# Chunk-select attention into soft MoE on one core: regrouped score blocks, a rearranged last batch, spare matmuls, and a second expert product in halves

## The chip, the core and the metric

The kernel runs on one core of a Trainium2 chip. A core has a matrix engine (TensorE, PE in the profile, with its weight loads shown apart as PEld), a vector engine (VectorE, DVE), a scalar engine (ScalarE, ACT), GpSimd (POOL) and SyncE (SP), which run their own instruction streams and wait for each other through semaphores. PE writes only to PSUM; DVE and ACT bring results from PSUM to SBUF. Sixteen DMA engines move data between HBM and SBUF. The metric is device time in microseconds (us) of one execution. Before the change it was 175.84 us (median of 3 runs, 175.56 to 177.19).

## The reference, cut to what matters

Attention over 4 batches x 8 heads of 768 rows and 64 columns, where each query row keeps only the 6 chunks of 32 keys with the largest upper bound of its score, followed by a soft mixture of experts over the 3072 x 512 result (8 experts, 4 slots each, hidden width 1024).

```python
k_min, k_max = k_chunks.min(3), k_chunks.max(3)             # 24 chunks of 32 keys
ub = sum(maximum(q * k_min, q * k_max))                     # per query row and chunk, causal
sel = top 6 chunks of ub
scores = where(sel & causal, scale * q @ k.T, -1e9)
attn = softmax(scores);  x = (attn @ v) as rows of (batch, position), 512 wide
logits = x @ phi                                            # 3072 x 32 slots
d = softmax of logits over the 3072 rows;  slot_input = d.T @ x
slot_out[e] = relu(slot_input[e] @ w1[e]) @ w2[e]           # 8 experts
c = softmax of logits over the 32 slots
out = c @ slot_out                                          # 3072 x 512, float32
```

## The kernel before

The work is a hand-written order (`manual_schedule`): each engine runs its instructions as the program lists them.

**The pair loop.** Two heads make a pair; there are 16 pairs, four per batch. Iteration `i` computes scores and exponentials of pair `i`, the upper bounds and the selection of pair `i+1`, the transposes of k and q of pair `i+2`, the product with v (`pv`) of pair `i-1`, and the normalised rows (`normalise`, `x_transposes`, `evac_x`) of pair `i-2`. The loads of k and q run four pairs ahead, those of v two pairs ahead, all of them and the expert weights as DMAs issued by POOL on one queue, so they land in the order of issue. Each `load_w` brings 1 MB (as it lies in SBUF), each k, q or v load 192 KB; `wplan` says how many weights an iteration issues. Weights 0 to 7 are of the first expert product and 8 to 15 of the second.

**Scores.** Because of causality a key block `kg` of 128 keys meets only the query blocks from `kg` on. `GROUPS` packs these blocks into six score tiles (`scores(i, g)`), each followed by one exponential on ACT (`expo`, line 297) and one `affine_select` on POOL (line 299) for the diagonal block. The score tiles rotate through two PSUM buffers of the pool `p_sc` (tag `sc`): a group's matmuls (line 272 for q and k, line 283 for the selection mask) wait until the exponential two groups earlier has read its buffer. Before the change the widths are 512, 512, 512, 512, 512 and 128 query columns per head. Results lie in `ep` (9 buffers) and, for the last group, `ep5`. `p_tp` (two buffers of one bank) and `p_at` (one of two banks) hold all other PSUM tiles.

**The soft MoE of a batch.** Once a batch's four pairs are transposed, PE computes its `moe_logits`, DVE copies them and takes a maximum per slot (`moe_copy`), PE transposes it (`moe_max`), DVE reduces it (`moe_bound`), PE spreads it over the partitions (`moe_exp`, first matmul), DVE updates the running maximum `m_run` and subtracts it (line 400), ACT takes the exponential `d_sb` (line 404), and PE adds up the slot inputs (`moe_dispatch`, line 435). `moe_comb` and `moe_ct` make the transposed combine weights. For batches 0 to 2 this is spread over the following loop iterations; for the last batch it stands alone behind the loop.

**The tail.** `pv` of the last pair is split into query blocks 0 to 3 and 4 to 5. After the last dispatch DVE writes the slot inputs (`siT_pad`), PE runs `experts_in` (line 617: four experts side by side, 128 x 32 weights, 512 columns), ACT the relu, PE the transposes `hidden_T`, then `experts_out` (line 652) into `so_ps` with `normalisers` (lines 638 and 640: 24 sums for the combine weights and one for the slot sums) between its halves, ACT `so_sb` (line 669), and 24 output products (line 680) that DVE and ACT scale by `cinv` and SP stores.

Of the kernel before, what the change touches and what calls it, by code (L numbers as in the profile page):

```python
# [18 lines left out]
CH = 32  # L19
# [12 lines left out]
    [(1, 0, 512, 0)],  # L32
    [(2, 0, 512, 0)],
    [(4, 0, 256, 0), (0, 512, 256, 256)],
    [(3, 0, 384, 0), (1, 512, 128, 384)],
    [(5, 0, 128, 0)],
]
# [9 lines left out]
def kernel(  # L47
# [60 lines left out]
    tp2 = i_ctx.enter_context(tc.tile_pool(name="tp2", bufs=2, side="right"))  # L108
    ep = i_ctx.enter_context(tc.tile_pool(name="ep", bufs=9, side="right"))
    ep5 = i_ctx.enter_context(tc.tile_pool(name="ep5", bufs=2, side="right"))  # L110
    tpu = u_ctx.enter_context(tc.tile_pool(name="tpu", bufs=2, side="right"))
# [61 lines left out]
    load_v(1)  # L173
    nc.gpsimd.dma_start(out=phi_sb, in_=moe_phi.rearrange("(hg p) s -> p hg s", p=P))
    make_identity(nc, identf)


# [113 lines left out]
    def expo(i, g):  # L291
        w = WIDTH[g]
        if g < 5:
            e = ep.tile([P, 2, 512], BF16, name="e_sb", tag="e_sb")
        else:
            e = ep5.tile([P, 2, P], BF16, name="e5_sb", tag="e5_sb")
        nc.scalar.activation(e[:, :, :w], st.pop(("scps", i, g))[:, :, :w], func=ACT.Exp, scale=scale)  # L297

        nc.gpsimd.affine_select(  # L299
            out=e[:, :, :P], in_=e[:, :, :P], compare_op=ALU.is_ge, fill=0.0,  # L300
            base=0, pattern=[[0, 2], [1, P]], channel_multiplier=-1,
        )
        st["e", i, g] = e

    def pv(i, ts):
        if i == LAST and ts[0] in (0, 4):
            st["at", i] = p_sc.tile([P, 2, 512], F32, name="at_ps", tag="sc")
        elif ts[0] == 0:
            st["at", i] = p_at.tile([P, 2, 512], F32, name="at_ps", tag="at")
        at = st["at", i]  # L310
        for t in ts:
            for h in range(2):
                o = at[:, h, t * (D + 1):(t + 1) * (D + 1)]
                for kg in range(t + 1):
                    g, c = BLOCK[(kg, t)]
                    nc.tensor.matmul(  # L316
                        o, lhsT=st["e", i, g][:, h, c:c + P], rhs=v_t[i % NV][:, h, kg, :],
                        start=(kg == 0), stop=(kg == t),
                    )

    def normalise(i, t0=0, t1=NQT, at=None):
        b, j = divmod(i, NPB)
        at = st.pop(("at", i)) if at is None else at
        at = at[:, :, :NQT * (D + 1)].rearrange("p h (t d) -> p h t d", t=NQT)[:, :, t0:t1]
        if j == 0:
            st["x", b] = xp.tile([P, NQT, H, D], BF16, name="x_sb", tag="x_sb")
        inv = tp2.tile([P, 2, NQT, 1], F32, name="inv", tag="inv")[:, :, t0:t1]
        nc.vector.reciprocal(inv, at[:, :, :, D:D + 1])
        nc.vector.tensor_tensor(  # L329
            st["x", b][:, t0:t1, 2 * j:2 * j + 2, :].rearrange("p t h d -> p h t d"),  # L330
            at[:, :, :, :D], inv.broadcast_to([P, 2, t1 - t0, D]), op=ALU.mult,
        )
# [18 lines left out]

    def moe_logits(b, hgs=range(NDG), home=(p_tp, "tp")):
        if hgs[0] == 0:
            st["lgps", b] = home[0].tile([P, NQT, NS], F32, name="lg_ps", tag=home[1])
        ps, xT = st["lgps", b], st["xT", b]
        for t in range(NQT):
            for hg in hgs:
                nc.tensor.matmul(
                    ps[:, t, :], lhsT=xT[:, hg, t * P:(t + 1) * P], rhs=phi_sb[:, hg, :],
                    start=(hg == 0 and t == 0), stop=(hg == NDG - 1 and t == NQT - 1),  # L360
                )

    def moe_copy(b):
        lg = small.tile([P, NQT, NS], F32, name="lg", tag="lg")
        pm = small.tile([P, NS], F32, name="pm", tag="pm")
        ps = st.pop(("lgps", b))
        if b == B - 1:
            nc.vector.tensor_reduce(pm, ps.rearrange("p t s -> p s t"), axis=AX.X, op=ALU.max)
            nc.scalar.copy(lg, ps)
        else:  # L370
            nc.vector.tensor_copy(lg, ps)
            nc.vector.tensor_reduce(pm, lg.rearrange("p t s -> p s t"), axis=AX.X, op=ALU.max)
        st["lg", b], st["pm", b] = lg, pm
# [14 lines left out]
    def moe_exp(b):  # L388
# [17 lines left out]
        if b > 0:  # L406

            dm = small.tile([P, 1, NS], F32, name="dm", tag="dm")
            nc.vector.tensor_tensor(dm[:, 0, :], m_old, m_new, op=ALU.subtract)
            nc.scalar.activation(dm, dm, func=ACT.Exp)  # L410
            if b == B - 1:
                moe_comb(b)
            nc.vector.tensor_tensor(si_acc, si_acc, dm.broadcast_to([P, NDG + 1, NS]), op=ALU.mult)
# [50 lines left out]
    wplan = {i: 1 for i in range(-1, NPAIR)}  # L464
    for i in (2, 5, 8, 11):
        wplan[i] = 0
    for i in (12, 13):
        wplan[i] = 2
    nw = 1
# [7 lines left out]
    for i in range(-2, NPAIR):  # L477
# [15 lines left out]
        if have(i + 1):  # L493
            select(i + 1)
        if have(i + 2):
            transposes(i + 2, "k")
# [17 lines left out]
        if have(i - 1):  # L514
            pv(i - 1, [3])
        if have(i + 2):
# [12 lines left out]
        if have(i):  # L529
            scores(i, 4)  # L530
            expo(i, 4)
            scores(i, 5)
            expo(i, 5)
        if have(i + 1) and i >= 0:
            ns_transposes(i + 1)
            evac_ns(i + 1)
        if have(i - 1):
            pv(i - 1, [4])
        moe(moe_dispatch, i - 3)
        if have(i - 1):  # L540
            pv(i - 1, [5])
# [17 lines left out]
    siT_pad = pads.tile([P, NDG, E, CH], BF16, name="siT_pad")  # L559
    hT_pad = pads.tile([P, NFG, E, CH], BF16, name="hT_pad")  # L560
    normalise(LAST - 1)
    pv(LAST, [0, 1, 2, 3])
    at_a = st["at", LAST]
    x_transposes(LAST - 1)
    evac_x(LAST - 1, copy=nc.scalar.copy)
    normalise(LAST, 0, 4, at_a)
    pv(LAST, [4, 5])
    moe_logits(B - 1, range(NDG - 1), (p_at, "at"))
    x_transposes(LAST, 0, 4)
    evac_x(LAST, 0, 4, nc.scalar.copy)  # L570
    normalise(LAST, 4, NQT)
    x_transposes(LAST, 4, NQT)
    evac_x(LAST, 4, NQT)
    moe_logits(B - 1, range(NDG - 1, NDG))
    nc.gpsimd.memset(siT_pad, 0.0)
    nc.gpsimd.memset(hT_pad, 0.0)
    i_ctx.close()
    moe_copy(B - 1)
    moe_max(B - 1)
    moe_bound(B - 1)  # L580
    moe_exp(B - 1)
    moe_dispatch(B - 1)


    tail = ctx.enter_context(tc.tile_pool(name="tail", bufs=1))
    op = ctx.enter_context(tc.tile_pool(name="op", bufs=5))
# [10 lines left out]
    for g in range(2):  # L597
# [5 lines left out]
        )  # L603
    moe_ct(B - 1)
    cinv = tail.tile([P, B * NQT], F32, name="cinv")
# [3 lines left out]
    h_sb = tail.tile([P, 2, 512], BF16, name="h_sb")  # L609
    so_sb = tail.tile([P, Dm], BF16, name="so_sb")  # L610
    h_ps = [p_sc.tile([P, 2, 512], F32, name=f"h_ps{f}", tag="sc") for f in range(2)]

# [21 lines left out]

    def normalisers():
        ps = p_tp.tile([P, B * NQT + 1], F32, name="cs_ps", tag="tp")
        for n in range(B * NQT):
            nc.tensor.matmul(
                ps[:, n:n + 1], lhsT=cT[:, n // 2, n % 2], rhs=ones_sq[:, :1], start=True, stop=True)
        nc.tensor.matmul(  # L640
            ps[:, B * NQT:], lhsT=zrow.rearrange("p j s -> p (j s)"), rhs=identf[:1, :1], start=True, stop=True)
        nc.vector.reciprocal(zinv, ps[:, B * NQT:])
        nc.vector.reciprocal(cinv, ps[:, :B * NQT])

    so_ps = p_at.tile([P, 2, 512], F32, name="so_ps", tag="at")

    def experts_out(f):
        for g in range(2):
            for fg in range(f * 4, (f + 1) * 4):
                for j in range(4):  # L650
                    e = g * 4 + j
                    nc.tensor.matmul(  # L652
                        so_ps[j * CH:(j + 1) * CH, 0, :], lhsT=hT_pad[:, fg, e, :],
                        rhs=w_sb[E + e][:, fg * Dm:(fg + 1) * Dm],
                        start=(g == 0 and fg == 0), stop=(g == 1 and fg == NFG - 1),
                    )

    experts_in(0, 0)
    experts_in(0, 1)
    relu(0)  # L660
# [3 lines left out]
    relu(1)  # L664
    experts_out(0)
    hidden_T(1)
    normalisers()
    experts_out(1)
    nc.scalar.activation(so_sb, so_ps[:, 0, :], func=ACT.Copy, scale=zinv)

# [3 lines left out]
    for m in range(B * NQT // 2):  # L674
        o_sb = op.tile([P, 2, Dm], F32, name="o_sb", tag="o_sb")
        rows = out[m * 2 * P:(m + 1) * 2 * P, :].rearrange("(p x) d -> p x d", x=2)
        for x in range(2):
            pool, tag = homes[n % 5]
            o_ps = pool.tile([P, Dm], F32, name="o_ps", tag=tag)
            nc.tensor.matmul(o_ps, lhsT=cT[:, m, x], rhs=so_sb, start=True, stop=True)  # L680
            if x == 0:
                nc.vector.tensor_scalar_mul(o_sb[:, x, :], o_ps, cinv[:, n:n + 1])  # L682
# [37 lines left out]
```

## Time and profile before

| | |
|---|---|
| median of 3 runs | 175.84 us |
| profiled execution | 176.33 us, of which 174.6 us from the first to the last instruction |
| busy time | PE 136.6 us (78%), DVE 124.8 (71%), ACT 120.5 (69%), POOL 98.8 (57%) |
| DMA | 26.25 MB in on the queue that POOL feeds, 6.29 MB out |
| chain that ended last, by engine | PE 36%, ACT 21%, DMA 15%, DVE 14%, POOL 6% |

The chain is followed back from the last instruction: at each step to whatever released it, or to the instruction before it on its engine. The execution has four stages. Up to about 14.8 us the first pairs are loaded and transposed. From 14.82 us (first exponential) to 134.54 us (end of the last) the pair loop runs, about 6.85 us for a pair without MoE work. From there to 156.20 us the tail runs from the last `pv` to the first store. The last 18.4 us are the stores. A line of the timeline below has start, duration, engine, source line, operation, tiles and count; the bracket behind it is how long the engine sat idle before it and what released it. A wait line has the time in total, the number of waits and the longest.

### The profile page before, as it was taken

What the parts mean: (1) busy time and instruction counts of PE and PEld (TensorE: products, weight loads), DVE (VectorE), ACT (ScalarE), POOL (GpSimd) and SP (SyncE); (2) the same over time, 40 slices, a digit from 0 to 9 for tenths busy, and PEclk for the clock granted to TensorE, in tenths of its full rate; (3) what the DMA queues carried; (4) which work ended last, traced back from release to release, by engine and by line L of the source; (5) the groups of instructions that cost most, each with busy time, mean ns of one, the idle gap of its engine ahead of it and who ended that gap; (6) DMA issues with size and microseconds to landing.
All of it is one profiled execution on the core that took longest, in us unless ns stands there. A gap on an engine that the chain in (4) does not pass through costs nothing.

```text
span 174.6 us, 6281 instructions
## 1 busy us (share of the span) xinstructions
PE 136.6 (78%) x2629; PEld 100.3 (57%) x2630; DVE 124.8 (71%) x430; ACT 120.5 (69%) x163; POOL 98.8 (57%) x192
## 2 busy tenths in 40 slices
PE   0459698999799789999988899999688669976410
PEld 0346476777577568877776777777567543532100
DVE  3467869999689888999987899999653560247530
ACT  2356998988789678988977698897667321156430
POOL 7995869869578457877775586659345500000000
PEclk9999999999999999999999999999999956999855
DMA  3999999999999999999999999199999994009995
GB/s 48 164 152 187 190 211 195 211 196 206 184 208 197 209 190 158 211 167 207 168 144 207 182 202 148 14 186 212 197 213 216 216 215 88 4 8 400 406 403 226
DMA packets 40460, 32.94 MB, mean 189 GB/s; under 512 B 26352, under 2 KB 34544, under 8 KB 40432
## 3 DMA queue, kind: packets, MB, share of 16 engines
q0 software_dynamic: 38416, 26.25, 102.4%
q1 hardware_dynamic: 2016, 6.29, 9.1%
q8 instruction: 20, 0.33, 0.7%
q14 instruction: 8, 0.07, 0.1%
HBM read 52.49 MB, written 6.29 MB: 337 GB/s over the span
## 4 chain that ended last, share of the span: by engine, by line
PE 36%; ACT 21%; DMA 15%; DVE 14%; POOL 6%; issue 4%; SPq 0%; ACTq 0%; POOLq 0%; DVEq 0%
ACT e_sb L297 14%; DMA k_in<-in_k_dram 10%; PE sc_ps L272 6%; DMA out_dram<-o_sb 5%; PE tr_ps L184 4%; PE sc_ps L283 4%; PE at_ps L316 4%; PE h_ps L617 3%; ACT kT L193 3%; POOL e_sb L299 3%; PE ub_ps L231 2%; DVE x_sb L329 2%; PE so_ps L652 2%; PE ub_ps L227 2%; DVE mm L202 2%
## 5 line engine op out<-in xcount | busy, mean ns | idle before, releaser
L297 ACT ACTIVATE e_sb<-sc_ps 128x1024 bf16<-128x1024 f32 x96 | 83.7, 937 | 10.5 <-PE sc_ps L283 10.5
L299 POOL TENSOR_SCALAR_AFFINE_SELECT e_sb<-e_sb 128x256 bf16<-128x256 bf16 x96 | 39.4, 422 | 33.5 <-ACT e_sb L297 32.9
L272 PE MATMUL sc_ps<-qT,kT 64*128 64x512 bf16 (+3 forms) x256 | 39.7, 310 | 7.6 <-ACT e_sb L297 7.4
L283 PE MATMUL sc_ps<-nsT,smask 64*128 64x256 bf16 (+1 forms) x448 | 37.1, 245 | 0.0
L316 PE MATMUL at_ps<-v_t,e_sb 128*128 128x65 bf16 x672 | 29.4, 194 | 1.1 <-DVE x_sb L329 1.1
L283 PEld LDWEIGHTS <-smask 64*128 64x128 bf16 x448 | 23.0, 95 | 7.3 <-issue 0.5
L316 PEld LDWEIGHTS <-e_sb 128*128 128x128 bf16 x672 | 25.1, 98 | 2.9 <-DVE x_sb L329 1.1
L272 PEld LDWEIGHTS <-kT 64*128 64x128 bf16 x256 | 15.4, 94 | 13.3 <-issue 8.3
L243 DVE MAX8 mx<-ub_ps 128x8 f32<-128x8 f32 (+2 forms) x192 | 17.0, 161 | 6.1 <-PE ub_ps L231 5.0
L202 DVE TENSOR_REDUCE mm<-kT 128x24 bf16<-128x768 bf16 x16 | 15.2, 951 | 6.1 <-ACT kT L193 5.1
L134 POOL DMA_DIRECT2D v_t<-in_v_dram x16 | 16.7, 1046 | 2.0 <-PE ns_ps L254 1.3
L193 ACT COPY kT<-tr_ps 128x768 bf16<-128x768 bf16 x16 | 12.8, 803 | 6.0 <-PE tr_ps L184 5.9
L329 DVE TENSOR_TENSOR x_sb<-at_ps,inv 128x768 bf16<-128x768 f32 (+2 forms) x17 | 15.5, 911 | 0.6
L208 DVE TENSOR_REDUCE mm<-kT 128x24 bf16<-128x768 bf16 x16 | 15.1, 942 | 0.0
L184 PE MATMUL tr_ps<-ident,k_in 128*64 128x128 bf16 x192 | 9.4, 240 | 7.1 <-DMA k_in<-in_k_dram 6.1
L193 ACT COPY qT<-tr_ps 128x768 bf16<-128x768 bf16 x16 | 13.2, 828 | 2.0 <-PE tr_ps L184 2.0
L682 DVE TENSOR_SCALAR o_sb<-o_ps,cinv 128x512 f32<-128x512 f32 x12 | 8.6, 748 | 6.9 <-DMA out_dram<-o_sb 3.7
L129 POOL DMA_DIRECT2D k_in<-in_k_dram x16 | 11.7, 728 | 1.6 <-POOLq L704 0.8
L231 PE MATMUL ub_ps<-bd,qpn 128*128 128x48 bf16 x192 | 10.3, 187 | 2.5 <-DVE qpn L218 2.3
L684 ACT ACTIVATE o_sb<-o_ps,cinv 128x512 f32<-128x512 f32 x12 | 7.8, 688 | 5.4 <-DMA out_dram<-o_sb 4.2
L129 POOL DMA_DIRECT2D q_in<-in_q_dram x16 | 11.5, 721 | 0.0
L122 POOL DMA_DIRECT2D w_sb<-in_moe_w_dram x16 | 11.4, 714 | 0.0
(96 smaller groups left out, 202.9 us busy)
## 6 DMA issues: line engine op xcount, KB each, us to landing
w_sb<-in_moe_w_dram POOLq DMA_DIRECT2D x16, 1024.0 KB, 13.1
out_dram<-o_sb SPq DMA_DIRECT2D x10, 512.0 KB, 5.2
k_in<-in_k_dram POOLq DMA_DIRECT2D x16, 192.0 KB, 7.4
q_in<-in_q_dram POOLq DMA_DIRECT2D x16, 192.0 KB, 7.6
v_t<-in_v_dram POOLq DMA_DIRECT2D x16, 192.0 KB, 9.4
out_dram<-o_sb SPq DMA_DIRECT2D x4, 256.0 KB, 3.3
phi_sb<-in_moe_phi_dram POOLq DMA_DIRECT2D x1, 32.0 KB, 10.1
```

The lines of the kernel that those rows point to most:

```text
L129: nc.gpsimd.dma_start(out=t, in_=src.rearrange("h (p g) d -> p h (g d)", p=P))
L134: nc.gpsimd.dma_start(out=v_t[i % NV][:, :, :, :D], in_=v[b, 2 * j:2 * j + 2].rearrange("h (g p) d -> p h g d", p=P),)
L184: nc.tensor.matmul(ps[h * 64:(h + 1) * 64, g, :], lhsT=src[:, h, g * D:(g + 1) * D], rhs=ident, is_transpose=True,)
L193: nc.scalar.copy(t.rearrange("d (p g) -> d p g", g=NQT), st.pop((nm + "ps", i)).rearrange("d g p -> d p g"),)
L202: nc.vector.tensor_reduce(mm[:, 0, 0, :], kT, axis=AX.X, op=ALU.min)
L243: nc.vector.max(mx[:, a, :], ub[:, a, :max(8, 4 * t + 4)])
L272: nc.tensor.matmul(ps[:, h, c:c + w], lhsT=kT[r, kg * P:(kg + 1) * P], rhs=qT[r, qs], start=True, stop=False,)
L283: nc.tensor.matmul(ps[:, h].rearrange("p (k y) -> p k y", y=P)[:, k0:k0 + 2 * m - 1:2, :], lhsT=smask[r, f % 2, kg].rearrange("p a b -> p ...
L297: nc.scalar.activation(e[:, :, :w], st.pop(("scps", i, g))[:, :, :w], func=ACT.Exp, scale=scale)
L299: nc.gpsimd.affine_select(out=e[:, :, :P], in_=e[:, :, :P], compare_op=ALU.is_ge, fill=0.0, base=0, pattern=[[0, 2], [1, P]], channel_mult ...
L316: nc.tensor.matmul(o, lhsT=st["e", i, g][:, h, c:c + P], rhs=v_t[i % NV][:, h, kg, :], start=(kg == 0), stop=(kg == t),)
L329: nc.vector.tensor_tensor(st["x", b][:, t0:t1, 2 * j:2 * j + 2, :].rearrange("p t h d -> p h t d"), at[:, :, :, :D], inv.broadcast_to([P, ...
```

## The change

- `GROUPS`: the widths become 512, 512, 384, 384, 512 and 384. The blocks are the same; two pieces are cut otherwise, so there is one piece more per pair. `ep` gets 5 buffers of 512, a new `ep3` 6 of 384.
- The load of `phi` and the making of `identf` move from the prologue into iteration -1, behind `select(0)`, ahead of `load(3)`.
- `wplan`: iterations 1 and 3 issue no weight and all others one. Before, 2, 5, 8 and 11 issued none, and 12 and 13 two.
- In the last iteration `pv(14)` is done earlier: block 4 with block 3, and block 5 between the scores of groups 4 and 5.
- Behind the loop the last pair's `pv` is split 0 to 2 and 3 to 5. The logits of the last batch are made twice, as `lg1` (kept as they are) and as `lg2`, whose accumulation stays open. The running maximum is put beside the transposed maxima as one more column, so one reduction gives the negated new maximum `mneg`; a matmul adds it into `lg2`, and ACT takes the exponential straight from PSUM. Maximum, copy and subtraction on DVE (lines 398 and 400) and the copy on ACT (line 369) are gone from this batch.
- `keep(n)` issues `n` matmuls of 512 columns into a part of a PSUM buffer that nobody reads; there are five in all.
- `moe_ct` of the last batch moves behind the first quarter of `experts_in`.
- `experts_out` makes its two halves of 256 columns in separate banks, in an order that ends the first half early; `so_sb` is written in two halves, and each output product is two matmuls. The slot sum (`zsum`) and the 24 combine sums (`csums`) are apart, the latter behind the last expert matmul. The first output tile is scaled in two halves.

```diff
@@ GROUPS
-    [(2, 0, 512, 0)],
-    [(4, 0, 256, 0), (0, 512, 256, 256)],
+    [(2, 0, 384, 0)],
+    [(4, 0, 256, 0), (2, 384, 128, 256)],
     [(3, 0, 384, 0), (1, 512, 128, 384)],
-    [(5, 0, 128, 0)],
+    [(5, 0, 128, 0), (0, 512, 256, 128)],
...
-    ep = i_ctx.enter_context(tc.tile_pool(name="ep", bufs=9, side="right"))
-    ep5 = i_ctx.enter_context(tc.tile_pool(name="ep5", bufs=2, side="right"))
+    ep = i_ctx.enter_context(tc.tile_pool(name="ep", bufs=5, side="right"))
+    ep3 = i_ctx.enter_context(tc.tile_pool(name="ep3", bufs=6, side="right"))
@@ pv
-        if i == LAST and ts[0] in (0, 4):
+        if i == LAST and ts[0] == 0:
+            st["at", i] = p_tp.tile([P, 2, 3 * (D + 1)], F32, name="at_ps", tag="tp")
+        elif i == LAST and ts[0] == 3:
             st["at", i] = p_sc.tile([P, 2, 512], F32, name="at_ps", tag="sc")
...
-    for i in (2, 5, 8, 11):
+    for i in (1, 3):
         wplan[i] = 0
-    for i in (12, 13):
-        wplan[i] = 2
@@ loop
+        if i == -1:
+            nc.gpsimd.dma_start(out=phi_sb, in_=moe_phi.rearrange("(hg p) s -> p hg s", p=P))
+            make_identity(nc, identf)
...
-            pv(i - 1, [3])
+            pv(i - 1, [3] if i < LAST else [3, 4])
...
             expo(i, 4)
+            if i == LAST:
+                pv(i - 1, [5])
             scores(i, 5)
@@ behind the loop
-    pv(LAST, [0, 1, 2, 3])
+    pv(LAST, [0, 1, 2])
     at_a = st["at", LAST]
+    pv(LAST, [3])
+    at_b = st["at", LAST]
     x_transposes(LAST - 1)
     evac_x(LAST - 1, copy=nc.scalar.copy)
-    normalise(LAST, 0, 4, at_a)
+    normalise(LAST, 0, 3, at_a)
     pv(LAST, [4, 5])
...
+    def keep(n):
+        for _ in range(n):
+            nc.tensor.matmul(h_ps[0][:, 1, :], lhsT=ident, rhs=w_sb[0][:, :512], start=True, stop=True)
+
+    moe_logits(BL, range(NDG - 1), lg1)
+    x_transposes(LAST, 0, 3)
+    evac_x(LAST, 0, 3, nc.scalar.copy)
+    normalise(LAST, 3, NQT, at_b)
...
+    moe_logits(BL, range(NDG - 1), lg2, False)
+    x_transposes(LAST, 3, NQT)
+    evac_x(LAST, 3, NQT)
+    keep(2)
+    moe_logits(BL, range(NDG - 1, NDG), lg1)
...
+    nc.vector.tensor_reduce(pm, lg1.rearrange("p t s -> p s t"), axis=AX.X, op=ALU.max)
+    moe_logits(BL, range(NDG - 1, NDG), lg2, False)
+    pmT = p_tp.tile([NS, P + 1], F32, name="pmT_ps", tag="tp")
+    nc.tensor.matmul(pmT[:, P:], lhsT=m_old[:1, :], rhs=identf[:1, :1], start=True, stop=True)
+    nc.tensor.matmul(pmT[:, :P], lhsT=pm, rhs=identf, is_transpose=True)
+    mneg = small.tile([NS, 1], F32, name="mb", tag="mb")
+    nc.vector.tensor_reduce(mneg, pmT, axis=AX.X, op=ALU.max, negate=True)
+    keep(2)
+    rep = identf[:NS, :NS].rearrange("p (o s) -> p o s", o=1)
+    nc.tensor.matmul(
+        lg2, lhsT=mneg.broadcast_to([NS, P]), rhs=rep.broadcast_to([NS, NQT, NS]), start=False, stop=True,
+    )
...
+    nc.scalar.activation(d_sb, lg2, func=ACT.Exp)
...
+    keep(1)
+    moe_dispatch(BL)
...
     experts_in(0, 0)
+    moe_ct(B - 1)
     experts_in(0, 1)
...
-    experts_out(0)
+    experts_out(0, [0], [0, 1])
     hidden_T(1)
-    normalisers()
-    experts_out(1)
-    nc.scalar.activation(so_sb, so_ps[:, 0, :], func=ACT.Copy, scale=zinv)
+    zsum()
+    experts_out(0, [1], [0, 1])
+    experts_out(1, [0, 1], [0])
+    nc.scalar.activation(so_sb[0], so_ps[0], func=ACT.Copy, scale=zinv)
+    experts_out(1, [0, 1], [1])
+    nc.scalar.activation(so_sb[1], so_ps[1], func=ACT.Copy, scale=zinv)
+    csums()
...
+            for y in range(2):
+                nc.tensor.matmul(halves[y], lhsT=cT[:, m, x], rhs=so_sb[y], start=True, stop=True)
+            if n == 0:
+                for y in range(2):
+                    nc.vector.tensor_scalar_mul(o_sb[:, x, y * HD:(y + 1) * HD], halves[y], cinv[:, n:n + 1])
```

## The prediction

> **What bounds the kernel now.** I read the busy time by stage first, then ACT's waits, then the timeline where two pairs meet, then the chain that ended last. The stages are one pair without MoE work, the last batch's softmax, and the start of the experts; after each engine's busy time stand the granted PE clock and the DMA share:
>
> ```profile
> core 0: us, PE busy (x) PEld busy (x) DVE busy (x) ACT busy (x) POOL busy (x), PEclk, DMA share, GB/s
> 77.13:83.98 6.85, 6.48 (x140) 5.12 (x141) 6.39 (x24) 6.37 (x9) 5.13 (x10) 1.00 1.25 198
> 139.00:143.30 4.30, 2.34 (x40) 1.90 (x39) 2.65 (x12) 1.26 (x5) 0.00 (x0) 0.67 1.07 215
> 143.30:146.00 2.70, 2.70 (x29) 1.07 (x32) 0.56 (x1) 0.00 (x0) 0.00 (x0) 0.50 0.96 194
> ```
>
> In a pair three engines are nearly full: removing one engine's wait soon meets the next one. In the softmax no engine is full, it is a chain of small steps, and the clock is halved just before the experts' dense matmuls. ACT's largest wait is for scores:
>
> ```profile
> ACT e_sb L297 <- PE sc_ps L283: 10.5, 18, 1.5
> ```
>
> Where two pairs meet it is 0.48 us a time:
>
> ```profile
> 73.45 1.37 ACT L297 ACTIVATE e_sb<-sc_ps 128x1024 bf16<-128x1024 f32 x2
> 74.60 0.39 PE L272 MATMUL sc_ps<-qT,kT 64*128 64x512 bf16 x2 [0.36 <-ACT e_sb L297]
> 75.30 1.94 ACT L297 ACTIVATE e_sb<-sc_ps 128x1024 bf16<-128x1024 f32 x2 [0.48 <-PE sc_ps L283]
> 76.30 1.06 DVE L243 MAX8 mx<-ub_ps 128x8 f32<-128x8 f32 x12 [0.25 <-PE ub_ps L231]
> ```
>
> The last two exponentials (1024 and 256 elements) take 1.37 us. PE may write group 0 of the next pair only when the larger is done (74.60), ACT can read it at 75.30, and the small one in between covers too little of these 0.70 us. DVE, by contrast, waits only 0.25 us. The chain shows the DMA queue and the tail (start, duration, what):
>
> ```profile
> 32.00 13.26 DMA k_in<-in_k_dram
> ...
> 134.80 0.97 DVE x_sb L329
> ...
> 139.04 0.37 DVE pm L368
> ...
> 140.11 0.42 PE bc_ps L391 x2
> ...
> 140.84 0.37 DVE ld L400
> ...
> 141.24 0.37 ACT d_sb L404
> 141.65 0.96 PE si_ps L435 x30
> 142.61 0.77 PE cT_ps L449 x6
> 143.38 4.64 PE h_ps L617 x34
> 148.03 0.35 PE hT_ps L629 x4
> 148.38 0.98 PE h_ps L617 x16
> 149.35 1.73 PE so_ps L652 x32
> ...
> 151.43 0.58 PE cs_ps L638 x24
> ...
> 152.31 1.87 PE so_ps L652 x32
> ```
>
> 34 expert matmuls take 4.64 us at the low clock, 16 take 0.98 once it is back.
>
> **Score groups.** An exponential takes 1038 ns on 1024 elements and 432 on 256, so on a line 0.84 us on 768; per pair 5 x 1.038 + 0.432 = 5.62 before and 3 x 1.038 + 3 x 0.836 = 5.62 after. The last one now covers the 0.70 us, so ACT can lose its 0.48 us. PE gets one piece more: two score and two mask matmuls with their loads, but the same columns. Those of the last piece of group 4 (two and two of 128 columns) take 0.30 us with their wait, so the price lies between 0 and 0.3; I take 0.05, as only issue is added. PE's 6.48 + 0.05 fits. What is late next is DVE: 6.85 - 0.25 = 6.60 us a pair, its 6.39 us of busy time plus gaps between instructions. So I take 0.25 us a pair, with 0 and 0.48 as bounds. By pairs, then. Pair 0: PE waited 1.06 us for ACT at 21.99 and DVE has room, 0.40. Pairs 1 to 3: DVE's slack is still to be used up, 0.35 + 0.30 + 0.25. Pairs 7 to 9 and 11 to 13: 6 x 0.25 = 1.5. Pairs 5, 6, 10 and 14 took 7.73, 9.44, 10.24 and 8.65 us; their extra time is DVE's eight or more MoE steps, or PE's dispatch, 0.
>
> **Weights.** The landing times of the single transfers show one queue: with a full queue k needs 0.98 us, q 1.02, v 1.50 and a weight 4.6 to 5.0, so 8.2 a pair with a weight against 6.85 of work. k of pair 5 landed at 37.14, behind the same transfers as after the change, and its copy (0.61 us later, by pair 6's 45.26 and 45.87) cannot start before 37.75. Before, it started at 38.17: of the 1.05 us won by then, 0.42 stay. Pair 6's k, the 13.26 above, landed behind weight 3; now weight 3 is issued a pair later, k lands at 37.14 + 1.02 + 1.50 + 0.98 = 40.64, and pair 4, which took 8.08 with the wait, takes 6.60: 1.48. Each weight issue (0.70 us on POOL) moves with its weight; POOL has 1.7 us free a pair. From there on every pair brings a weight, and the queue fills: q of pair 6 is down at 41.66, v and weight 3 behind it take 6.15, pair 7 (no weight) 3.5, pairs 8 to 14 8.2 each, and k of pair 15 lands at 41.66 + 6.15 + 3.5 + 57.4 + 0.98 = 109.7. It is wanted at about 111.0 (iteration 13 began at 113.13, less the 3.4 won, plus 1.23 to the transposes). This cover is thin, 1.3 us. It also caps a faster loop at 113.13 + 1.23 - 109.7 = 4.7 us up to there. The last weight landed at 147.37; with the queue's idle time gone it lands near 139, wanted at about 143. phi and identf (0.76 + 0.52 us on POOL) go ahead of k of pair 3, its q and weight 1; that k landed at 21.22 because the queue was busy to 20.69, so nothing; without that cover, 1.3 us.
>
> Loop: 0.42 + 0.25 + 1.48 + 1.5 = 3.65, less 0.25 because ten PV matmuls now precede group 4's scores in the last pair: **3.4 us** (bounds 1.0, where pairs keep 6.85 and only the k wait goes, and 5.0, by the cap).
>
> **Tail up to the dispatch.** Count from T, the end of the last exponential (134.54 before); the dispatch began at T + 7.11. PV of pair 14 now ends before T, so x_sb (0.97) leaves the path. From T: the diagonal select 0.56, 22 PV matmuls 0.87 (1.45), 18 logits 0.56 (2.0), three transposes 0.25, the 18 second logits 0.56 (2.85; new on the path), three transposes 0.30, a 384-element copy 0.36 between the rows of 0.29 (256) and 0.55 (768) and its hand-over (3.55), six logits 0.33, pm 0.37 (4.35), pmT 0.30, the maximum 0.29 (5.05), the addition into lg2, exponential 0.37, dispatch. The addition over 192 float columns has no row: at least the 0.42 of 32 columns, at most 0.9 (three times pmT's 128 columns); 0.55, nearer to pmT's 0.30. That is T + 6.1: **1.0 us** (0.4 to 1.3). Gone are m_run 0.20 and ld 0.37. The five spare matmuls are 0.22 us each (32 of 512 columns, four abreast, take 1.73, so 512 columns 0.216): two lie under the copy, two under the maximum (0.05 too long), one under the exponential. Without cover, at half clock, they cost up to 0.9, since the maximum's addition is queued behind them on PE.
>
> **Clock, dispatch and experts.** I take the clock as held. In the records of PE I summed columns, 512 to 0.216 us, over the 3.4 us stretches in which the clock changes: it fell after stretches filled to 20% (137.05 to 140.46) and 25% (160.94), and held at 44% (123.39). The new chain, with spare matmuls, second logits and the wide addition, comes to some 50%. The dispatch then takes the 0.74 it took at 66.23 instead of 0.96, and siT 0.49 instead of cT's 0.77: 1.24 against 1.66, **0.4**. From the first expert matmul to the last was 10.9 us (143.31 to 154.2). After: four quarters of h 4 x 0.87, cT 0.35, hidden_T 2 x 0.35, zsum 0.31, second product 3.6 = 8.45: **2.45**, of which 2.0 is clock (half of 143.31 to 147.28). The second product doubles its matmuls at equal columns: 0, or +1.1 if each costs the 37 ns of a PV matmul; the dispatch's 25 ns says 0.
>
> [...]
>
> **First store.** csums 0.60, cinv 0.38, then two half tiles of 0.42 against so_sb 0.70, product 0.45 and 0.75: 1.9 against 2.0, **0.1**. The 18.4 us of stores are bound by DMA at 400 GB/s and stay.
>
> **Sum.** 3.4 + 1.0 + 0.4 + 2.45 + 0.1 = 7.35 off the profiled 176.33 gives 169.0; that execution lay 0.49 above the median, so I forecast a median of 168.5.
>
> **Rivals.** *The clock falls all the same*: 2.0 + 0.22 (dispatch) + 0.1 (spare matmuls) come back, 170.8. For it: the stretches are not tied to the program and 44% is the only filling near 50 that was seen. *DVE is not the floor*: its qpn row takes 0.35 to 0.91 us, median 0.79, and other phases may cost less; pairs then run at ACT's 6.4 until k of pair 15 caps the gain, 1.5 more, 167.0 and at best 166. *The queue decides, and the kernel is slower*: with a weight in every pair from 4 on, k of pairs 12 to 15 comes late, PE stands at the k transposes, and the scores queued behind them with it. Each percent longer per transfer costs 0.7 us over the 70 us from 40 to 110, after the first 2%. It decides against the change from 12% (a weight at 5.3): 0.7 x 10 = 7 us, 176. Single weights took 4.4 to 5.9 us, the mean 4.9; hence a small chance, and a larger one for a partial delay, 169.5 to 174.
>
> **How the numbers follow.** Forecast 0.50 (its own range 167 to 170), clock lost 0.17, faster pairs 0.15, partial delay 0.12, slower by the queue 0.06. The range 165.9 to 172.8 leaves out the slower case and most of the far end of the partial one. A measurement here tells about 1% from no change: faster 0.90, within 0.04, slower 0.06.
>
> **What would show it.** Pairs 7 to 9 at about 6.60 us with DVE's waits gone and ACT's at about 0.2; pair 4 without a k wait; k of pair 15 landing near 109.7; the dispatch 6.1 us after the last exponential; a granted clock of 1.00 up to the stores, and 16 expert matmuls in 0.87. Wrong: pairs at 6.85, PE waiting for k_in after 80 us, or a clock of 0.50 under the experts.

## The result, and the profile after

| | before | after |
|---|---|---|
| median | 175.86 us (20 runs) | 174.2 us (20 runs) |
| profiled execution, of it span | 176.33, 174.6 | 174.59, 172.9 |
| last exponential ends (T) | 134.54 | 135.75 |
| T to dispatch | 7.11 | 5.61 |
| dispatch to first expert matmul | 1.66 | 1.27 |
| first to last expert matmul | 10.9 | 9.68 |
| from there to the first store | 2.0 | 2.1 |
| the stores | 18.4 | 18.5 |

The ratio is 0.9878, 95% interval 0.9849 to 0.9907: 1.2% faster, where 4.2% was forecast. The medians are of all executions; the ratio leaves out those more than 1.5% above the fastest of their kernel, eight of the 20 after the change. The tail gained more than foreseen up to the dispatch and less under the experts. The loop, which was to end 3.4 us earlier, ends 1.2 us later.

The stages after (start and end, length, busy time and count of each engine, clock, DMA share): a pair without MoE work, the stretch from T to the dispatch, the dispatch, the experts.

```profile
core 0: us, PE busy (x) PEld busy (x) DVE busy (x) ACT busy (x) POOL busy (x), PEclk, DMA share, GB/s
74.17:80.71 6.54, 6.45 (x142) 5.06 (x141) 6.44 (x23) 6.49 (x8) 5.72 (x12) 1.00 1.40 201
135.75:141.36 5.61, 5.30 (x99) 4.03 (x97) 2.90 (x10) 1.63 (x4) 3.19 (x4) 1.00 0.38 77
141.36:142.63 1.27, 0.90 (x30) 0.80 (x29) 0.75 (x5) 0.65 (x3) 0.00 (x0) 1.00 0.05 13
142.63:152.31 9.68, 9.10 (x211) 5.97 (x212) 1.53 (x9) 1.67 (x3) 0.00 (x0) 1.00 0.01 2
```

The pair takes 6.54 us against 6.85, with DVE, ACT and PE all nearly full, and the clock stays at 1.00. The chain of the changed kernel (start, duration) shows the meeting of two pairs and one of the places where the loop lost:

```profile
72.38 1.73 ACT e_sb L294 x2
74.17 0.66 ACT e_sb L294
75.09 1.02 ACT e_sb L294
...
86.12 0.70 PE at_ps L315 x22
87.07 1.01 issue
88.08 0.53 PE lg_ps L357 x14
...
118.67 0.52 PE lg_ps L357 x21
119.19 1.11 issue
```

The last exponential of a pair ends at 74.11 and the next pair's first starts at 74.17: the 0.48 us wait is gone. But for 1.01 and 1.11 us PE stands idle with nothing released to it, between logits matmuls of one accumulation. PE's timeline has a third such place, between PV matmuls, the largest:

```profile
54.41 0.67 PE L315 MATMUL at_ps<-v_t,e_sb 128*128 128x65 bf16 x16
56.80 0.22 PE L315 MATMUL at_ps<-v_t,e_sb 128*128 128x65 bf16 x2 [1.72 <-issue]
56.86 0.75 PE L357 MATMUL lg_ps<-phi_sb,xT_sb 128*128 128x32 bf16 x24
57.55 0.39 PE L269 MATMUL sc_ps<-qT,kT 64*128 64x512 bf16 x2
```

In each case the next pair's first scores are queued behind. ACT waits for them, and DVE for the logits. The changed kernel's waits, with total, number and longest:

```profile
ACT e_sb L294 <- PE sc_ps L280: 7.6, 6, 2.5
...
DVE lg L365 <- PE lg_ps L357: 3.9, 3, 1.7
...
PEld L357 <- issue: 2.3, 2, 1.2
PEld L315 <- issue: 2.2, 2, 1.8
```

Before, ACT's 10.5 us were 18 waits of up to 1.5 us; now they are 6, three of them the 2.50, 1.80 and 1.88 us at 58.26, 89.24 and 121.17 us, in iterations 5, 9 and 13, those with a batch's logits. Most of what the loop lost passes through these three: in a kernel without the stalls (experiment 10) the first two are 0.62 us each and the third is gone. Of the kind "issue" PE's matmuls have one such wait in the loop before, of 0.56 us:

```profile
58.16 0.20 PE L358 MATMUL lg_ps<-phi_sb,xT_sb 128*128 128x32 bf16 x2 [0.56 <-issue]
```

The chain through the tail, for comparison with that of before:

```profile
136.28 0.81 ACT xT_sb L348
137.14 0.56 PE lgt_ps L357 x16
140.36 0.53 PE lg_ps L599 x2
141.36 0.92 PE si_ps L427 x30
142.63 1.05 PE h_ps L655 x16
144.12 1.84 PE h_ps L655 x32
146.31 0.98 PE h_ps L655 x16
147.28 0.87 PE so_ps L695 x32
148.81 1.89 PE so_ps L695 x64
150.72 0.48 ACT so_sb L714
151.25 1.06 PE so_ps L695 x32
152.31 0.69 PE cs_ps L682 x24
```

The expert matmuls run at 16 in about 1 us throughout, where 34 took 4.64 us; maximum, subtraction and their hand-overs are gone from the softmax, and a step of ACT has come between the matmuls of the second product.

**What PE waits for.** Count PE's instructions in the order of its program, from 0: matmuls, weight loads and the few semaphore instructions among them. PE stops ahead of numbers 1729, 3009 and 4289, and before the change ahead of 1729. These are 1280, or 5 x 256, apart. The expectations below count without the semaphore instructions and with 255 to a block; they call the three places 1720, 2994 and 4268 (or 4266), and these names are kept. The profile's page lists a DMA queue of its own kind (packets, MB, share of the engines):

```profile
q8 instruction: 22, 0.36, 0.8%
```

It moves packets of 16 KB: 22 for the 22 ends of 256 instructions that PE crosses in this count, from number 193 on, and 20 for 20 before the change. They are read here as fetches of PE's program, a block of 256 instructions each. All 23 idle times of PE's matmuls of more than 0.25 us without a releaser, in the loops of the 13 kernels profiled for this document, stand at block ends counted so, those behind spare instructions too. For each block end the trace gives when PE crossed the end before it, when the fetch of the next block started, and when PE went on at its first instruction:

| kernel, block | end before crossed | fetch starts | delay | PE goes on | after start | PE idle |
|---|---|---|---|---|---|---|
| after, 1720 | 49.81 | 54.52 | 4.71 | 56.80 | 2.28 | 1.72 |
| after, 2994 | 81.79 | 85.83 | 4.04 | 88.08 | 2.25 | 1.01 |
| after, 4268 | 114.01 | 118.01 | 4.00 | 120.30 | 2.29 | 1.11 |
| after, 5287 (weights landed) | 141.71 | 142.37 | 0.66 | 148.54 | 6.17 | none |
| before, 1720 | 52.10 | 55.72 | 3.61 | 58.16 | 2.45 | 0.56 |
| before, 2230 | 65.98 | 66.66 | 0.68 | 71.49 | 4.83 | none |

In the changed kernel the queue of loads is full up to the last weight (landed 139.9), and in the loop a fetch starts 2.9 to 5.3 us after the block end; once all loads had landed it started 0.66 and 0.70 us after it (141.71 and 148.54), and in the kernel before 0.68 us after the end at 65.98, where no weight was under way. From start to first use it took at least 2.25 us in the changed kernel's loop. So at the three places the block took 6.3 to 7.0 us. Without the stall PE would have used it up in 5.2 to 5.3 (6.99 - 1.72 = 5.27, and 5.28 and 5.18), since a logits iteration adds 48 short matmuls and loads to the pair's 283 instructions.

### The profile page after: what moved, and what is told of

The parts are those of the page before. It is cut to its first block, busy times and chain, and to the rows that moved or that the text cites. A ratio compares the mean times of both kernels' runs of the same rounds, so it can differ in the third digit from the quotient of the medians.

```text
span 172.9 us, 6648 instructions
## 1 busy us (share of the span) xinstructions
PE 137.6 (80%) x2815; PEld 105.0 (61%) x2815; DVE 123.4 (71%) x429; ACT 122.5 (71%) x163; POOL 99.0 (57%) x192
## 4 chain that ended last, share of the span: by engine, by line
ACT 30%; PE 29%; DVE 15%; DMA 14%; issue 6%; POOL 1%; DVEq 0%; ACTq 0%; POOLq 0%
ACT e_sb L294 22%; DMA k_in<-in_k_dram 9%; DMA out_dram<-o_sb 5%; PE tr_ps L181 4%; PE at_ps L315 4%; ACT kT L190 4%; PE sc_ps L269 3%; ACT qT L190 2%; PE h_ps L655 2%; PE so_ps L695 2%; PE sc_ps L280 2%; DVE mm L199 2%; DVE mm L205 2%; DVE x_sb L328 2%; PE lg_ps L357 1%
## 5 line engine op out<-in xcount | busy, mean ns | idle before, releaser
L294 ACT ACTIVATE e_sb<-sc_ps 128x1024 bf16<-128x1024 f32 (+1 forms) x96 | 82.8, 917 | 9.3 <-PE sc_ps L280 7.6
L296 POOL TENSOR_SCALAR_AFFINE_SELECT e_sb<-e_sb 128x256 bf16<-128x256 bf16 x96 | 38.6, 415 | 33.7 <-ACT e_sb L294 33.3
L269 PE MATMUL sc_ps<-qT,kT 64*128 64x128 bf16 (+3 forms) x288 | 39.5, 294 | 4.1 <-ACT e_sb L294 2.5
L280 PE MATMUL sc_ps<-nsT,smask 64*128 64x128 bf16 (+1 forms) x480 | 36.8, 239 | 0.0
L315 PE MATMUL at_ps<-v_t,e_sb 128*128 128x65 bf16 x672 | 30.0, 194 | 3.0 <-issue 1.7
L280 PEld LDWEIGHTS <-smask 64*128 64x128 bf16 x480 | 24.5, 95 | 6.2 <-issue 0.5
L269 PEld LDWEIGHTS <-kT 64*128 64x128 bf16 x288 | 16.3, 94 | 10.7 <-issue 6.6
L328 DVE TENSOR_TENSOR x_sb<-at_ps,inv 128x768 bf16<-128x768 f32 (+1 forms) x17 | 15.5, 910 | 0.6
L181 PEld LDWEIGHTS <-k_in 128*64 128x64 bf16 x192 | 6.6, 116 | 7.9 <-DMA k_in<-in_k_dram 6.3
```

The lines of the kernel that those rows point to most:

```text
L181: nc.tensor.matmul(ps[h * 64:(h + 1) * 64, g, :], lhsT=src[:, h, g * D:(g + 1) * D], rhs=ident, is_transpose=True,)
L269: nc.tensor.matmul(ps[:, h, c:c + w], lhsT=kT[r, kg * P:(kg + 1) * P], rhs=qT[r, qs], start=True, stop=False,)
L280: nc.tensor.matmul(ps[:, h].rearrange("p (k y) -> p k y", y=P)[:, k0:k0 + 2 * m - 1:2, :], lhsT=smask[r, f % 2, kg].rearrange("p a b -> p ...
L296: nc.gpsimd.affine_select(out=e[:, :, :P], in_=e[:, :, :P], compare_op=ALU.is_ge, fill=0.0, base=0, pattern=[[0, 2], [1, P]], channel_mult ...
L315: nc.tensor.matmul(o, lhsT=st["e", i, g][:, h, c:c + P], rhs=v_t[i % NV][:, h, kg, :], start=(kg == 0), stop=(kg == t),)
L328: nc.vector.tensor_tensor(st["x", b][:, t0:t1, 2 * j:2 * j + 2, :].rearrange("p t h d -> p h t d"), at[:, :, :, :D], inv.broadcast_to([P, ...
```

## The experiments

Four theories. **A, place:** what counts is only where the block ends fall; the eight instructions more in every pair (two score and two mask matmuls with their loads) shifted them, from 44 instructions behind the first logits matmul to four ahead of it in iteration 5. **B, engines:** the pairs are too full for PE and its neighbours, and any disturbance shows. **C, queue:** the full queue of loads holds PE up as such. **D, fetch:** the fetch of PE's instructions waits behind the loads. A gap below is an idle time of PE's matmuls in the loop that nothing released, of more than 0.25 us. T is, as above, the end of the last exponential. Profiled times belong to one execution; ratios are to the kernel before on the same chip.

**1. Eight PE instructions more per pair in the kernel before.** The spare matmuls write columns of group 5's tile that nobody reads.

```diff
+        if g == 5:
+            for h in (0, 1, 0, 1):
+                r = slice(h * 64, (h + 1) * 64)
+                nc.tensor.matmul(
+                    ps[:, h, 256:384], lhsT=kT[r, :P], rhs=qT[r, :P], start=True, stop=True,
+                )
```

> The kernel before with four spare matmuls (128 columns, into a part of the score tile that nobody reads) in group 5 of every pair: eight more PE instructions a pair, as many as the change adds, with the old widths and the old order of weights. Theory A (PE's instructions arrive in blocks of about 255, and PE runs dry where a block ends among the short PV and logits matmuls): the first logits matmul of batches 0, 1 and 2 stands at instructions 1724, 2974 and 4224 as in the changed kernel, so PE idles without a releaser there, about 1.7, 1.0 and 1.1 us near 57, 88 and 120 us, and the time rises from 175.9 to 178.5 to 179.5. Rival B (the pairs are too full after regrouping, so each MoE pair falls behind): no such gaps beyond the 0.56 us of before, time within 0.5. Rival C (the DMA queue, now full throughout, holds PE up): as B, since the weights are as before.

Measured: 176.06 us against 175.94, ratio 1.0016 (0.998 to 1.0051). The same instruction numbers in the same iterations cost nothing that can be measured, so A alone is out. In the kernel before, pairs end later and at times no weight is under way (none from 63.81 to 66.88, with a fetch 0.68 us after the block end at 65.98), so B, C and D stand. The profiled execution is the longest of the ten, 178.17 us. It has four gaps, of 0.67, 0.33, 0.50 and 0.33 us, all at block ends and two of them at 2994 and 4268; whether an execution of usual length has them was not profiled.

**2. The changed kernel with the old score groups**, buffers too.

```diff
-    [(2, 0, 384, 0)],
-    [(4, 0, 256, 0), (2, 384, 128, 256)],
+    [(2, 0, 512, 0)],
+    [(4, 0, 256, 0), (0, 512, 256, 256)],
     [(3, 0, 384, 0), (1, 512, 128, 384)],
-    [(5, 0, 128, 0), (0, 512, 256, 128)],
+    [(5, 0, 128, 0)],
```

> The changed kernel with the old widths 512, 512, 512, 512, 512, 128 and the old buffers for them; all else as changed. A: the logits stand at 1676, 2894 and 4112 as before, so only the first gap is left, 0.5 us; pairs go back to 6.85 us; the last exponential ends near 133.5 (135.75 in the changed kernel), time 171.5 to 172.5. B: also about 172, as the pairs are less full. C: the gaps of 1.7, 1.0 and 1.1 us stay, as the queue is as full as in the changed kernel, and the slower pairs come on top, 175.5 to 177.

Measured: 172.26 us, ratio 0.9782 (0.9732 to 0.9832), T at 133.09, no gap. C, by which the gaps were to stay, fails; A and B had both forecast about this time. Without the regrouping the change is about 1% faster than with it (0.9782 against 0.9878, and the intervals do not meet): the part meant for the loop cost time, and pairs of 6.85 us (66.84 to 73.69) without stalls beat pairs of 6.54 with three.

**3. and 4. Spare one-column matmuls ahead of the loop**, 77 in one kernel and 32 in another, which move all block ends back by so many matmuls and loads (here the kernel with 77).

```diff
+    def spare(n):
+        ps = p_at.tile([P, 2, 512], F32, name="sp_ps", tag="at")
+        for _ in range(n):
+            nc.tensor.matmul(ps[:, 0, :1], lhsT=ones_sq, rhs=ones_sq[:, :1], start=True, stop=True)
+
+    spare(40)
     for i in range(-2, NPAIR):
...
+        if i == -1:
+            spare(37)
```

> The changed kernel with 77 spare one-column matmuls in PE's waits of the first 9 us, 154 instructions, so that the block ends lie 97, 121 and 143 instructions behind the first logits matmul of batches 0, 1 and 2 (before: 44, 100 and 154; changed: 4 ahead, 20 and 42 behind). Nothing in the loop changes. A: the three gaps of 1.7, 1.0 and 1.1 us vanish, the last exponential ends near 132, time 170 to 171. [...] B and C: gaps and time as in the changed kernel, 174.2 within 0.7.

Measured: 170.78 us, ratio 0.9703 (0.9645 to 0.9762), T at 132.08, two gaps of 0.30 and 0.29 us.

> The changed kernel with 32 such matmuls (64 instructions) ahead of the first transposes: the block ends move to 68, 44 and 22 instructions ahead of the first logits matmul. A: the gaps stay in the same three pairs but begin that much earlier in the order, among the last scores and the PV matmuls; time 173 to 176. B and C: gaps where they are in the changed kernel, at 4 ahead, 20 and 42 behind.

Measured: 170.97 us, ratio 0.9714 (0.9657 to 0.977), T at 131.53, one gap of 0.33 us. A's forecast for 77 held and that for 32 failed: two placements, one of which should have kept the gaps, lose them nearly alike. B and C, by which nothing was to change, fail with both. In the kernel with 32 the fetch of the block at 1720 started 2.87 us after the end before it (47.47, 50.34) and left 3.04 us until use (53.38). So how long a fetch waits differs from kernel to kernel, and it, not the place alone, decides.

**5. The changed kernel with the old distribution of the weights.**

```diff
-    for i in (1, 3):
+    for i in (2, 5, 8, 11):
         wplan[i] = 0
+    for i in (12, 13):
+        wplan[i] = 2
```

> The changed kernel with the order of weights of before (none in iterations 2, 5, 8, 11, two in 12 and 13). Theory A (only the place of a block end counts): the three gaps of 1.7, 1.0 and 1.1 us stay at instructions 1720, 2994 and 4266; with pair 4's wait for k back, 174.5 to 175.5. Theory D (PE's next block of instructions, 16 KB, is fetched through the DMA engines and waits there behind the weights; the fetch starts 0.2 to 0.6 us after a block end where the queue is empty and 2 to 5 us after it where it is full): the queue is full near 54 and 118 and nearly empty near 85, so the first and third gap stay, 0.8 to 1.7 us, and the second goes; 173.5 to 174.5.

Measured: 173.23 us, ratio 0.9892 (0.981 to 0.9974); gaps of 0.94 at 2994 and 0.42 at 4266, none at 1720, T at 133.87. Moving the loads moves the gaps, with PE's program as it was; which of them would go was forecast wrongly. At 1720 the fetch waited 2.26 us instead of 4.71.

**6. No weight in the iterations ahead of the logits** (1, 4, 8 and 12), three in 13.

```diff
-    for i in (1, 3):
+    for i in (1, 4, 8, 12):
         wplan[i] = 0
+    wplan[13] = 3
```

> The changed kernel with no weight in iterations 1, 4, 8 and 12 and three in 13, so that the queue runs empty before the block ends in the logits iterations 5, 9 and 13. The same instructions on every engine otherwise. A: gaps as in the changed kernel, 174.2 within 0.7. D: fetches start within about 2 us of the former block end there, each gap is below 0.5 us, the last exponential ends near 132.5 (135.75), time 170.5 to 172. The last weight lands later, near 143; wanted at about 143.5, up to 0.5 us may be lost to it.

Measured: 172.14 us, ratio 0.9831 (0.9765 to 0.9896). Only the third gap went: its fetch started 0.76 us after the block end (112.92, 113.68). At the other two the queue was still full with older loads; from 30 us to 91 us the transfers landed 6 to 14 us after their issue. Fetches began 3.94 and 3.89 us late, and gaps of 0.90 and 1.01 us remained. Leaving out one weight does not empty a queue this far behind.

**7. The load taken off the queue, PE's program unchanged.** From the third on, each weight is loaded to a sixth, and the expert matmuls read the first two weights only, so the experts' part of the output is another one.

```diff
+        if i >= 2:
+            src, dst = src[:, :1, :F], dst[:, :1, :F]
         nc.gpsimd.dma_start(out=dst, in_=src)
...
-                    rhs=w_sb[e][:, dg * F + f * 512:dg * F + (f + 1) * 512],
+                    rhs=w_sb[0][:, dg * F + f * 512:dg * F + (f + 1) * 512],
...
-                        rhs=w_sb[E + e][:, fg * Dm + y * HD:fg * Dm + (y + 1) * HD],
+                        rhs=w_sb[1][:, fg * Dm + y * HD:fg * Dm + (y + 1) * HD],
```

> The changed kernel with the same instructions of PE at the same rows, but every weight from the third on loaded to a sixth (one row group and 1024 of its columns), and all expert matmuls reading the first two weights; the experts' output is so another one. It takes the load off the DMA queue in the loop and nothing else. Instruction fetch behind the weights: the fetch of each block of PE's instructions starts 0.1 to 1.0 us after PE has crossed the end of the block before, instead of 2.3 to 5.6, and PE's idle times without a releaser at rows 1720, 2994 and 4268 are gone or below 0.4 us; the pair before iteration 5 has no wait for k, T (end of the last exponential) near 135.75 - 0.9 - 3.5 = 131.3, median 169 to 171. Place of the block ends alone: the rows have not moved, so the three idle times stay at 1.0 to 1.7 us, T near 134.8, median 173. Pairs too full for the engines: ACT's waits of 1.8 to 2.5 us in iterations 5, 9 and 13 stay.

Measured: 169.01 us, ratio 0.9629 (0.9582 to 0.9676), T at 130.45, no gap. PE's timeline of this kernel where the changed one stood for 1.72 us:

```profile
53.37 0.86 PE L317 MATMUL at_ps<-v_t,e_sb 128*128 128x65 bf16 x22
54.07 0.75 PE L359 MATMUL lg_ps<-phi_sb,xT_sb 128*128 128x32 bf16 x24
54.76 0.39 PE L271 MATMUL sc_ps<-qT,kT 64*128 64x512 bf16 x2
```

All 22 PV matmuls run without a break, over the same block end. The fetches for the three blocks started 0.73, 2.06 and 1.81 us after the end before (48.89 and 49.62, 78.75 and 80.81, 109.97 and 111.78) and left 4.38, 3.05 and 3.20 us; PE used the three blocks up in 5.11, 5.11 and 5.01 us. The 0.1 to 1.0 expected was too narrow, perhaps because k, q and v are still loaded in each pair, which was not tried apart. But with the same program at the same numbers all gaps are gone, and most of the waits of iterations 5, 9 and 13 with them: those pairs take 7.11, 7.11 and 7.11 us instead of 9.08, 8.53 and 8.55. This leaves D: A fixes the places and they did not move; B's engines have the same work. C without the fetch does not say why every gap, in every kernel, stands at the end of a block of 256 instructions, and the loads themselves were waited for only at pair 5's k.

**8. The second product's halves in two PSUM tiles** instead of two banks of one.

```diff
-    so_t = p_at.tile([P, 2, 512], F32, name="so_ps", tag="at")
-    so_ps = [so_t[:, y, :HD] for y in range(2)]
+    so_t = [p_at.tile([P, 2, 512], F32, name="so_ps0", tag="at"), p_sc.tile([P, 2, 512], F32, name="so_ps1", tag="sc")]
+    so_ps = [so_t[y][:, 0, :HD] for y in range(2)]
```

> The changed kernel with the two halves of the second expert product in two PSUM tiles instead of two banks of one. If PE's 0.58 us wait for the first half's copy at 151.25 is only that one tile is tracked as a whole: the wait goes, the last expert matmul ends about 9.2 us after the first instead of 9.7, first store and time 0.5 us earlier (173.7). Rival: the combine sums, cinv or the stores are late next, and less than 0.2 us is left of it.

Measured: 172.88 us, ratio 0.9861 (0.979 to 0.9933). First to last expert matmul fell from 9.68 to 8.90 us. PE's timeline of the changed kernel, then the chain with the split:

```profile
148.74 1.93 PE L695 MATMUL so_ps<-w_sb,hT_pad 128*32 128x256 bf16 x64
151.25 1.06 PE L695 MATMUL so_ps<-w_sb,hT_pad 128*32 128x256 bf16 x32 [0.58 <-ACT so_sb L714]
```

```profile
142.38 1.05 PE h_ps L655 x16
143.86 1.84 PE h_ps L655 x32
146.05 0.98 PE h_ps L655 x16
147.03 0.87 PE so_ps L695 x32
148.55 2.73 PE so_ps L695 x96
151.28 0.70 PE cs_ps L682 x24
```

In the changed kernel the second half's matmuls wait while ACT reads the first half: the two lie in one tile, and the matmuls wait 0.58 us for that read though they write another bank. In two tiles the 96 matmuls run through in 2.73 us. The difference in time, 1.3 us between medians on different comparisons, lies inside the intervals; the part in the tail is read from the chain. The loop of this run had its three gaps (1.45, 1.56 and 1.11).

**9. The changed kernel without the five spare matmuls.**

```diff
-    keep(2)
...
-    keep(2)
...
-    keep(1)
```

> The changed kernel without the five spare matmuls. If they hold the clock: it falls to 0.50 within 3 us of 140, 16 expert matmuls take 1.7 to 1.9 us instead of 1.0, and the time grows by 1.5 to 2.5 us to 176. If the second logits and the shorter chain hold it already: clock 1.00 to the stores, time 174.0 to 174.2.

Measured: 177.07 us (two executions), ratio 1.0104 (1.0009 to 1.02). Its stages under the first expert matmuls, and its chain:

```profile
140.53:143.94 3.41, 2.26 (x43) 1.83 (x47) 1.85 (x10) 0.99 (x4) 0.00 (x0) 1.00 0.02 5
143.94:147.35 3.41, 3.41 (x38) 1.33 (x30) 0.56 (x1) 0.00 (x0) 0.00 (x0) 0.50 0.00 0
```

```profile
143.60 1.62 PE h_ps L652 x16
145.96 2.53 PE h_ps L652 x28
148.84 0.98 PE h_ps L652 x16
```

The clock falls to 0.50 for one stretch of 3.41 us, and from the first expert matmul to the second product it takes 6.22 us (143.60 to 149.82) instead of 4.65. In the ten profiled kernels that keep the spare matmuls the clock stays at 1.00 from T to the stores, so they do hold it, as far as one profiled execution without them can tell. The loop of this run had its three gaps (1.44, 1.01, 1.39) and one of 0.43 more, T at 136.72.

**10. and 11. Both repairs together**: the two PSUM tiles, with 77 and with 32 spare one-column matmuls.

> The changed kernel with 77 one-column matmuls in the first 9 us and the second product's halves in two PSUM tiles. If the two losses are independent, they add: 170.8 less the 0.58 us of PE's wait (0.8 by first to last expert matmul) gives 170.0 to 170.4, ratio to before about 0.967; first to last expert matmul 8.9 us, no idle time of PE without a releaser above 0.4 us. If block ends fall badly again in the tail, 170.8 or more.

Measured: 170.13 us, ratio 0.9676 (0.9641 to 0.9712); T at 131.82, no gap, first to last expert matmul 8.91 us.

> The same with 32 one-column matmuls ahead of the loop instead of 77. By the single run of each part 171.0 - 0.8 = 170.2; by its profiled span (168.66, the shortest so far) rather 169.5 to 170. Which of the two counts of matmuls is better is not told by either theory; both are to be at or below 170.5.

Measured: 170.29 us, ratio 0.9652 (0.9612 to 0.9691); its profiled execution, the longest of the six at 172.06 us, had one gap, of 0.61 us. The two intervals overlap, so neither count is shown to be better. The two versions beat the kernel before by 3.2% and 3.5%, and by these ratios the changed one by about 2%.

## Why the prediction was right and wrong

**The step that failed** is in "Score groups": "PE gets one piece more", "I take 0.05, as only issue is added. PE's 6.48 + 0.05 fits". The busy time does fit, 6.45 of 6.54 us. What was left out is that PE's instructions are fetched too, and how late their fetch starts under the loads: 4.71, 4.04 and 4.00 us after the block end at the three places, and 0.73, 2.06 and 1.81 us with most of the load taken off (experiment 7). So denser and shorter pairs stood on one side, a queue kept full by "every pair brings a weight" on the other. The queue's filling was weighed only for the arrival of k. That the kernel is faster at all is owed to the tail. The price against the kernel without gaps (experiment 10) is 1.98 us in iteration 5 (9.08 against 7.10), 1.42 in 9 and 1.36 in 13, 4.8 together. T lies 3.9 later; the rest is given back in between, 0.5 of it in iteration 10 (10.24 against 10.76), for a reason that was not followed up. The row that could have told is in the profile of before: the 0.56 us of PE without a releaser at 58.16.

**The rest of the loop term** was right in mechanism and nearly in size. The pairs take 6.54 to 6.60 us (6.60 forecast); pair 4 has no wait for k; k of pair 5 landed at 37.04 (37.14) and left 0.67 us of the gain so far (0.42); k of pair 15 landed at 109.54 (109.7) and the last weight at 139.9 (near 139). With the gaps gone T is 131.82 in experiment 10 and 130.45 in 7, which is spared pair 5's k too, against 131.14. The last pair lost 0.42 instead of 0.25.

**Tail to the dispatch:** 5.61 instead of 6.1 after T, a gain of 1.5 where 1.0 was forecast. **Clock:** 1.00 to the stores, as taken; the chance of 0.17 for its fall belonged to a danger that is real without the spare matmuls (0.50 in experiment 9). Dispatch to first expert matmul took 1.27 (1.24).

**Experts:** 9.68 instead of 8.45. The four quarters of h took 1.05 + 1.84 + 0.98 = 3.87 for 3.48, cT 0.44 for 0.35, the second product 0.87 + 1.89 + 1.06 = 3.82 for 3.6, and 0.58 is the wait for `so_sb`, a wait that the change adds and that the working lacked. The doubled matmuls themselves cost at most the 0.2 by which the second product was longer. Experiment 8 shows the wait to come from the shared tile. The halves gained nothing in time to the first store (2.1 against 2.0).

The sum by stages: -1.2 + 1.5 + 0.4 + 1.2 - 0.1 - 0.1 = 1.7 us, the 174.6 - 172.9 of the spans. None of the rivals came: in a full pair DVE, ACT and PE are busy for 6.44, 6.49 and 6.45 of 6.54 us, so that no engine alone is the floor, and PE waited for no k behind 80 us. That the time lies next to the 169.5 to 174 of the partial delay is chance, as its mechanism, a late k, did not come.

## What to carry to other kernels

Where a change makes an engine's code denser and keeps the load queue full, compare the time in which the engine uses up a block (here 5.0 to 5.3 us for 256 instructions of PE) with the delay of the fetch and the time from its start to the first use (here 2.9 to 5.3 and at least 2.25 us), and look for idle time without a releaser at equal distances in its program (here 1280 instructions). The stalls of 1.72, 1.01 and 1.11 us changed with what shifted instructions (two of 0.30 and 0.29 left in experiment 3) and with what shifted transfers (0.94 and 0.42 in experiment 5), so a variant that is faster by some spare instructions may only have moved them. Taking load off the queue removed them here (no gap in experiment 7); fewer instructions should too, but this was not tried. The halves that were to overlap needed tiles of their own: in one tile the second waited 0.58 us, in two it did not.

## What the runs showed of the hardware that was not expected

- The 16 KB packet of a block took 0.89 to 1.33 us in the profiles before and after, and in the changed kernel's loop at least 2.25 us passed from its start to the first instruction of the block. It started 0.66 and 0.70 us after the block end before it once all loads had landed (142.37 and 149.24), but 2.9 to 5.3 us after it under the full queue. What in the queue it waits for was not tried.
- The clock fell to 0.50 after stretches of 3.41 us in which PE never waited for more than 1.92 us at a time. It did so in experiment 9 (longest wait 0.37 us, PE busy for 2.26 us by the profile), in the loop of experiment 8 (a gap of 1.56 us in the stretch that ended at 88.40, the clock 0.50 to 91.81) and in the loop of experiment 11 (a wait of 1.92 us for a k, the clock 0.50 from 39.54 to 42.95). In experiment 8 the stretch held one of the three fetch stalls; whether the stall cost the clock was not tried.
- An estimate of how full PE was in such stretches, from the profiles before and after: count each matmul with its columns, 512 to 0.216 us, times the share of 128 x 128 that its form in the trace fills. In the kernel before, the clock fell after stretches filled to 19% (137.05 to 140.46) and 25% (160.94 to 164.35) and stayed at 1.00 after one of 37% (89.26 to 92.67). In the changed kernel it fell after 26% (159.03 to 162.44) and stayed at 1.00 after 42% (87.35 to 90.77) and after the 43% of the stretch with spare matmuls (138.55 to 141.96). How a matmul's columns are spread over its time moves a stretch by some 2 points. No limit is shown by these few stretches.
